# A gated state-space and expert mixer on one core: a new static order, and openings of the inverse that TensorE may run

## The chip, the cores and the metric

The kernel runs on one core of one Trainium2 chip. The metric is device time in microseconds (us) of one execution; lower is better. The core has a matrix engine (TensorE, PE in the profile), a vector engine (VectorE, DVE), an activation engine (ScalarE, ACT), a general engine (GpSimd, POOL), and queues for DMA transfers, of which SyncE's (SP) carries nearly all. Each engine works off its own list of instructions in order and waits on semaphores for what other engines or transfers must deliver first. Operands lie in on-chip memory (SBUF, 128 partitions); matmuls write to PSUM, from which ACT or DVE must take the results away ("evict" them) before the place is used again.

## The reference

For `x = A_u` with 2048 tokens of 512 channels (bf16) the reference mixes two results with a gate per token:

```python
g = sigmoid((x * gate_w).sum(-1))
a = A(x, ...)   # convolution of each channel with a kernel of length 2048, + u * Dskip
b = B(x, ...)   # x, plus an expert's output at the two tokens with the largest score
return g * a + (1 - g) * b
```

In `A` the kernel of channel d is `K[d, l] = Re sum_n C[d,n] * dt[d] * B[d,n] * exp(dt[d] * A[d,n] * l)` with 128 states n; the causal convolution with it is done through FFTs. In `B` a score `x @ w_r` picks two of the 2048 tokens; for these a feed-forward network with 1792 hidden units, `(silu(xs @ w_gate) * (xs @ w_up)) @ w_down`, times the sigmoid of the score, is added to `x`.

## The kernel before

The convolution is done with blocks of 1024 tokens: two blocks of the input, two halves h of the channels (256 each). The stages are:

- `forward(blk)` (L876): transform of a block by matmuls with a table that is loaded from memory, 128 matmuls of 128x512 in 32 operations of four; the results, real and imaginary parts of four frequency tiles, are evicted to `X`.
- `tab1`, `tab2` (L691, L669, L471, L480, L456): for each half, the tables of `exp(dt*A*l)`: an argument by matmul, its fraction, a sine, a magnitude by exponential, and their products. These are DVE and ACT work.
- `kgen(h)` (L905): the kernel in time from these tables, 256 pairs of short matmuls for a half, evicted in pieces by ACT; then three selections (`sel`, L919 to L934) that bring it into the order in which it is transformed.
- `kspec(h)` (L961): the kernel's spectrum, by matmuls with tables `c_ksp` (five of 512 KB for each half), which must land first. In it the block that carries over from the other one is added: for h=0 by TensorE afterwards (L968), for h=1 ahead of the matmuls, either by ScalarE, which writes the scaled copy into PSUM (one ACTIVATE of 128x1024, L949), or by TensorE (two matmuls of 128x512, L968). Which one is a choice per operation.
- `products(h, ...)` (L456): complex products of input and kernel spectra on DVE, with some sums done on TensorE (L1007).
- `inverse(h)`: for each of 16 PSUM groups an opening operation writes `U * (1-g)/g` for two token blocks into PSUM (`sa`, ScalarE, two ACTIVATEs of 128x256, L1036); 16 matmuls (L1053) add the inverse transform of the products; and two evictions (L1061, ACT or DVE) multiply by g and write the output tile.
- `routing()`: transposes of the input (L747), scores (L760), two rounds of argmax with a transpose each for the value and the index (L778, L780), a gather by matmul with one-hot columns (L806), the expert's network with matmuls that have two columns (L824, L837), whose weights share SBUF with other buffers and are loaded late.

The program records 661 operations, an operation being one or several instructions of one engine. Nothing is scheduled at run time: `ORDER` is a string of three base-36 digits for every operation, which gives the order of all of them, and so each engine's list; `SECOND` says for each operation that has two engines as alternatives which one is used; `PLACES` says which PSUM or SBUF place a result takes. The costs beside the operations (`cost=...`) were used when these tables were made, and don't act in the program. A planner's times are therefore not visible in the kernel; its order is. An operation is put on an engine by helpers through which nearly all DVE and ACT work goes: `TT` (L456) two-operand DVE work, `EV` (L475) evictions and copies, `SCL` (L480) scaling, `AC` (L471) an activation function, `CP` (L467) small copies, `DMA` (L483).

Of the kernel before, what the change touches and what calls it, by code (L numbers as in the profile page):

```python
# [356 lines left out]
def small_mats():  # L357
# [14 lines left out]
ORDER = (  # L372
    "00301q00m00x00000200400q00r00s00600701c00500101a01k01b01n01o00h01m00i01l08d01e01d00t04n01v00u00v01y00802001w02108f00w02k08c07602400y00c01f07801u00d009"
    "02e01x02607702502c00z01z02d01002g02l02f02i02702h02j02802a02m00b02b00a07500l01102o02p02901p01s00j02n02q02r02z08e03004o05m01601t03103204p03307903401g04q"
    "03502s03603701707a03802t00g03904b01405l00o00p03n03q01h03b03a07b01203c03d04r07l07n03e03f05s07k01501801303g05n00e00f07m03h03i07c04t03j03k07o04u03r05p05o"
    "03l07p04v03m07q03x04s03y04x04w01901i03v07e07r03w03z05t07d04304107f07g05u04204y04008h07h04405004z05q04907i08g07j0510c10c00c204805w04704607s05200k05307t"
    "05v06004505404c05z05x0610c306705704a07v0c405506300n04d05y0c507u05607w04e03o07z06207x06406r0c906605906s07y0580860ca05b0c604f04i08204h02305a06805c084022"
    "04g04j06t05d05g06901r05e01j06a05h0800c703s08105f06d05i06e06k0c808506l08308906b06f06u05j0cb06v06m08w06n06o0a60cc06w06g0cd06p08b06h05k08y09a08x08706i0bs"
    "09b0880bu08a0a509j09d0bt0bv0ce06509c09e09009h09k08z09f06q06x0bw09g09t09105r09i0bx09209l09m0by09q09p09n09w03t09s02u09r09u0bz06j09v0cf06z09x0a70cg06y03p"
    "03u0ch09o08k07004k04l04m08i0720710ci08j02w0cj0a20ck08l0730cs0a30cm0a009y0a40cl09z0co08r0a109508m0ct08p08n08q0cn02v0cw0a80aa08s0ak0du0930ab0a908t0ac0al"  # L380
    "08o0960cp0ad0am0940ah08u0cq0dv0cr08v0ai0cu0ae0970cy0af0ax0cz0980aj0cv0990d00an0aw0ag0d20d30d50cx0d60d80d90b10dy0d10d40da0db0df0dh0d70dc0de0dd0b20dl0az"
    "02x0di0dx0b30dk0dg0ao0ap0740b40dj0b502y0b70ar0dm0dp0dq0dn0dr0do0b60ds0as06c0b80at0dw0fh0dt0au0av0aq0ff0fi0fr0fj0fk0fg0bd0fs0ba0fm0fn0fl0b90bb0fo0g90be"
    "0b00ga0e10bc0fp0bf0bh0fq0bg0bi0e30ge0gf0bk0ft0gg0gb0gc0e40fu0e80gd0bj0gi0e00bm0fw0ay0bl0g40fv0bn0e20e70gh0dz0ef0ei0ej0eg0e60bo0eq0er0ec0bp0br0eh0e50bq"
    "0e90ek0ep0es0ed0fz0g60ew0ee0ex0g10fx0ev0et0eu0ey0f80ea0gv0fy0hn0f50f60f90fa0f70f20g00ho0hj0gw0gt0ez0hs0hp0g50g20f00g70en0eb0h10h90g80g30f30el0gu0gz0gx"
    "0f10hk0fb0f40gy0h20hc0hl0h00h30h60eo0em0gk0fd0gj0gl0gn0fe0hm0gq0hd0he0hr0hq0ha0h40hx0gm0hb0h50hh0i50gp0i10ht0go0gs0i60gr0i20h70i70hi0hf0h80hg0i30fc0i8"
    "0ib0i40hu0hy0hz0hv0hw0ic0i00ia0i9"
)
# [13 lines left out]
def bass_gated_mix__ssm_conv_s4__moe_arch_mod__prompt_kernel(nc, A_u, A_A_re, A_A_im, A_B_re, A_B_im, A_C_re, A_C_im, A_log_dt, A_Dskip,  # L401
# [24 lines left out]
    with ExitStack() as es:  # L426
# [313 lines left out]
        def routing():  # L740
# [148 lines left out]
        def kgen(h):  # L889
            r = RW[h]  # L890
            for b0, ng in [(8 * i, 8) for i in range(8)]:
# [6 lines left out]
                for g0 in (0, np_):  # L898
                    def mm(hh, b0=b0, gs=range(g0, g0 + np_), pb=pb, np_=np_):
# [246 lines left out]
```

## Time and profile before

| | before |
|---|---|
| median of 3 runs | 151.04 us (150.5 to 151.19) |
| profiled execution | 150.42 us |
| its span, first to last instruction | 148.4 us |
| TensorE busy in the span | 132.8 us, 1723 matmuls |
| VectorE busy | 134.9 us, 199 instructions |
| ScalarE busy | 129.1 us, 210 instructions |
| mean granted TensorE clock | 0.976 of full speed |

The profiled execution is 2.02 us longer than its span, and lies 0.62 us below the median of the three runs. Three engines are busy for between 87% and 91% of the span, so the share of busy time alone doesn't say which of them sets the end; the views below go stage by stage. "Busy" is the union of an engine's instructions. An instruction's mean duration is a little longer than the step from its start to the next one's, since neighbours overlap; the chain of waits gives such steps.

### The profile page before, as it was taken

To read this page: it belongs to the slowest core of one execution; us is meant where nothing else is said; L and a number is where in the kernel's file an instruction comes from. 1 tells how busy PE (TensorE), PEld (TensorE's weight loads), DVE (VectorE), ACT (ScalarE), POOL (GpSimd) and SP (SyncE) were. 2 spreads that over 40 slices of the span, in tenths; PEclk is the share of its full clock that TensorE was granted. 3 is DMA by queue.
4 is the path that set the end of the run, shared out by engine and by line. 5 is a ranking of instruction groups with operands and counts; after the bars stand their busy time and mean duration, and the time that the engine had idled before them with its cause. 6 is when DMAs were issued, how large, how long until landed. Compare 5 with 4: busy or idle time off the path is not lost.

```text
span 148.4 us, 4019 instructions
## 1 busy us (share of the span) xinstructions
PE 132.8 (90%) x1723; PEld 99.8 (67%) x1723; DVE 134.9 (91%) x199; ACT 129.1 (87%) x210; POOL 5.6 (4%) x12
## 2 busy tenths in 40 slices
PE   0289977989999999999969989999999999999980
PEld 0168753766447544997538879968565888888870
DVE  1499999997998999996999999999979999999981
ACT  4689999996699999999998996679899999999540
POOL 8000000000000000000310000010000000000000
PEclk9999999985799999999999999999999999999999
DMA  3899299999700000740080695928800010106216
GB/s 97 265 363 403 94 311 402 406 382 514 324 0 4 0 0 12 246 175 4 0 255 33 181 382 183 383 49 345 325 6 2 4 38 0 35 4 177 84 57 177
DMA packets 13459, 24.93 MB, mean 168 GB/s; under 512 B 1359, under 2 KB 8290, under 8 KB 13282
## 3 DMA queue, kind: packets, MB, share of 16 engines
q1 hardware_dynamic: 12434, 24.03, 45.2%
q10 hardware_dynamic: 976, 0.66, 1.5%
q8 instruction: 13, 0.21, 0.5%
q14 instruction: 4, 0.03, 0.1%
q0 software_dynamic: 32, 0.00, 0.0%
HBM read 22.58 MB, written 4.20 MB: 181 GB/s over the span
## 4 chain that ended last, share of the span: by engine, by line
PE 72%; DMA 17%; DVE 6%; SPq 2%; issue 1%; ACT 0%
PE ps L1053 18%; PE ps L876 16%; PE ps L905 12%; PE ps L961 10%; DMA AR<-in_B_w_up_dram 10%; DMA AR<-c_ksp 5%; PE ps L1007 5%; PE ps L691 3%; DVE AR L456 2%; DMA AR<-in_A_B_im_dram 2%; SPq L483 2%; PE ps L747 2%; PE ps L968 1%; DVE AR L1061 1%; PE ps L760 1%; PE ps L824 1%
## 5 line engine op out<-in xcount | busy, mean ns | idle before, releaser
L456 DVE TENSOR_TENSOR AR<-AR 128x1024 bf16<-128x1024 bf16 (+13 forms) x135 | 118.1, 934 | 5.6 <-DMA AR<-in_A_B_im_dram 2.1
L475 ACT ACTIVATE AR<-ps 128x1024 bf16<-128x1024 f32 (+5 forms) x57 | 46.6, 863 | 5.2 <-PE ps L905 2.3
L876 PE MATMUL ps<-AR 128*128 128x512 bf16 x128 | 31.7, 395 | 0.0
L1053 PE MATMUL ps<-AR 128*128 128x256 bf16 x256 | 29.0, 273 | 0.0
L1053 PEld LDWEIGHTS ps<-AR 128*128 128x128 bf16 x256 | 25.1, 98 | 2.9
L471 ACT ACTIVATE AR<-ps 128x512 bf16<-128x512 f32 (+1 forms) x32 | 24.6, 822 | 2.3 <-PE ps L691 1.4
L876 PEld LDWEIGHTS ps<-AR 128*128 128x128 bf16 x128 | 12.4, 101 | 13.6 <-issue 1.5
L961 PE MATMUL ps<-AR 128*128 128x256 bf16 x160 | 19.3, 273 | 1.8 <-DMA AR<-c_ksp 1.8
L961 PEld LDWEIGHTS ps<-AR 128*128 128x128 bf16 x160 | 15.3, 98 | 5.6 <-DMA AR<-c_ksp 1.6
L905 PEld LDWEIGHTS ps<-AR 128*128 128x128 bf16 x512 | 17.8, 96 | 0.3
L905 PE MATMUL ps<-AR 128*128 128x84 bf16 (+1 forms) x512 | 17.9, 196 | 0.0
L1061 ACT ACTIVATE AR<-ps,AR 128x256 bf16<-128x256 f32 x27 | 11.6, 479 | 3.7 <-PE ps L1053 3.3
L1036 ACT ACTIVATE ps<-AR 128x256 f32<-128x256 bf16 x32 | 14.0, 493 | 0.1
L471 ACT ACTIVATE AR<-AR 128x1024 bf16<-128x1024 int16 (+5 forms) x16 | 12.7, 797 | 0.5 <-DMA AR<-in_A_log_dt_dram 0.3
L691 PE MATMUL ps<-AR 128*128 128x256 bf16 x64 | 10.1, 285 | 0.0
L480 ACT ACTIVATE AR<-ps 128x1024 bf16<-128x1024 f32 x8 | 8.2, 1030 | 0.9 <-PE ps L876 0.8
L591 PE MATMUL ps<-AR 128*128 128x128 bf16 x8 | 2.0, 472 | 7.1 <-DMA AR<-in_A_A_re_dram 4.5
L691 PEld LDWEIGHTS ps<-AR 128*128 128x128 bf16 x64 | 5.7, 99 | 3.2 <-ACT AR L475 0.6
L1007 PE MATMUL ps<-AR 128*128 128x512 bf16 x32 | 7.4, 379 | 0.0
L480 ACT ACTIVATE AR<-AR 128x256 int32<-128x256 f32 (+1 forms) x12 | 6.9, 585 | 0.0
L591 PEld LDWEIGHTS ps<-AR 128*128 128x128 bf16 x8 | 1.1, 170 | 7.6 <-DVE AR L458 4.4
L480 DVE TENSOR_SCALAR AR<-AR 128x256 int32<-128x256 f32 (+1 forms) x18 | 5.7, 327 | 0.4 <-ACT AR L471 0.4
(73 smaller groups left out, 91.3 us busy)
## 6 DMA issues: line engine op xcount, KB each, us to landing
AR<-c_ksp SPq DMA_DIRECT2D x10, 512.0 KB, 4.6
AR<-in_A_u_dram SPq DMA_DIRECT2D x4, 512.0 KB, 6.4
AR<-c_fwd SPq DMA_DIRECT2D x4, 512.0 KB, 11.8
AR<-out_dram SPq DMA_DIRECT2D x4, 512.0 KB, 6.1
AR<-c_inv SPq DMA_DIRECT2D x1, 2048.0 KB, 9.0
AR<-in_B_w_gate_dram SPq DMA_DIRECT2D x1, 1792.0 KB, 10.1
AR<-in_B_w_up_dram SPq DMA_DIRECT2D x1, 1792.0 KB, 14.6
out_dram<-AR SPq DMA_DIRECT2D x14, 128.0 KB, 2.2
```

Source lines behind the costliest of these rows:

```text
L456: return P.op(DVE, lambda h: h.tensor_tensor(out=o, in0=a, in1=b, op=op), rd, wr, cost=tt_cost(o, a, b), **k)
L471: return P.op(ACT, lambda h: h.activation(out=o, in_=a, func=func, scale=scale, bias=bias), rd, wr, cost=0.185 + nel(o) * 0.833e-3 + (0.09 ...
L475: return P.op((ACT, DVE), (lambda h: h.activation(out=o, in_=a, func=ACTF.Copy), lambda h: h.tensor_copy(o, a)), rd, wr, cost=cost or (0.1 ...
L480: return P.op((ACT, DVE), (lambda h: h.activation(out=o, in_=a, func=ACTF.Copy, scale=c), lambda h: h.tensor_scalar(out=o, in0=a, scalar1= ...
L691: last = hh.matmul(pb(0, 128, c * 256, (1, 256)), WP(0, 128, ((2 * h + q) * 4 + c) * 128, (1, 128)), MV(0, 128, a * 512 + f * 256, (1, 256 ...
L876: last = h.matmul(pb(0, 128, part * 512, (1, 512)), F[ft](0, 128, ((par * 4 + st) * 2 + part) * 128, (1, 128)), x, start=(pas + st == 0), ...
L905: last = hh.matmul(pb(0, 128, g // np_ * 512 + g % np_ * W4 + o, (1, n)), TP[h][1 - i // 2](0, 128, (b0 + g) * 128, (1, 128)), r[k](0, 128 ...
L961: last = hh.matmul(pb(0, 128, n * 256, (1, 256)), KP[h][u](0, 128, tau * 128, (1, 128)), KC[h](0, 128, jg * 256, (1, 256)), start=(k == 0 ...
L1007: r = hh.matmul(pb(0, 128, pm * 512, (1, W)), CB(0, 128, 128 * (k if part == 0 else 0), (1, 128)), b(0, 128, ((0, 3), (1, 2))[part][k] * 2 ...
L1036: last = hh.activation(out=pb(0, 128, e * 256, (1, 256)), in_=U(0, 128, tb * D + h * HC, (1, HC)), func=ACTF.Copy, bias=0.0, scale=SG(0, 1 ...
L1053: r = hh.matmul(pb(0, 128, e * 256, (1, 256)), G(0, 128, ((par * 2 + part) * 4 + ft) * 512 + (2 * t2 + e) * 128, (1, 128)), yv(h, blk, par ...
L1061: P.op((ACT, DVE), (lambda hh, o=o, i_=i_, g_=g_: hh.activation(out=o, in_=i_, func=ACTF.Copy, scale=g_), lambda hh, o=o, i_=i_, g_=g_: hh ...
```

## The change

The diff does five things.

1. `ORDER`, `SECOND` and `PLACES` are replaced: every engine gets a new order of its work, some operations with a choice change engines, and some results change places.
2. The planner's costs beside four kinds of operation are other numbers (the transposes of the parameters, 0.66 to 0.25 and 1.7 to 0.55; the short matmuls of `kgen`, 0.0343 to 0.0365 each). They don't act in the program.
3. A buffer `DGX` of 4 KB a partition holds 16 diagonal matrices of 128x128, the identity scaled per token by `(1-g)/g`. One new operation in `late()` writes it: one DVE multiplication (`dgd`) or 16 ACTIVATEs of 128x128 (`dga`).
4. A new small copy in `routing()` puts `(1-g)/g` into bf16 for that.
5. The opening of an inverse group may be done by TensorE (`sp`), with two matmuls that multiply `U` by such a diagonal, as well as by ScalarE (`sa`). Either way the operation now reads `DGX`, so it waits for the new operation of 3.

```diff
-ORDER = ( ... )   # 661 operations
+ORDER = ( ... )   # 663 operations
...
+        DGX = B("dgx", oF + 16 * KB, 4 * KB)
...
-            P.op(PE, pct, [PC, CBI], [bb], cost=0.66)
+            P.op(PE, pct, [PC, CBI], [bb], cost=0.25)
...
-            P.op(PE, wt, [(CM1, p), DG32], [(wp_, p)], cost=1.7)
+            P.op(PE, wt, [(CM1, p), DG32], [(wp_, p)], cost=0.55)
...
+            CP(SGB(0, 128, 64, (1, 16)), SG(0, 128, 96, (1, 16)), [(SG, "x")], [(SGB, "x")])
...
         def late():
+            def dgd(hh):
+                return hh.tensor_tensor(out=DGX(0, 128, 0, (128, 16), (1, 128)), in0=CB(0, 128, 0, (0, 16), (1, 128)), in1=SGB(0, 128, 64, (1, 16), (0, 128)), op=MUL)
+            def dga(hh):
+                r = None
+                for k in range(16):
+                    r = hh.activation(out=DGX(0, 128, k * 128, (1, 128)), in_=CB(0, 128, 0, (1, 128)), func=ACTF.Copy, bias=0.0, scale=SG(0, 128, 96 + k, (1, 1)))
+                return r
+            P.op((DVE, ACT), (dgd, dga), [CBI, (SGB, "x"), (SG, "x")], [DGX], cost=(2.25, 5.2))
...
-                    P.op(PE, mm, kd, [(pb, g0)], cost=np_ * 4 * 0.0343)
+                    P.op(PE, mm, kd, [(pb, g0)], cost=np_ * 4 * 0.0365)
...
-                        P.op(ACT, sa, [(SG, "x")] + [(U, (tb, h)) for tb in tbs(t2, par)], [pb], cost=0.88)
+                        def sp(hh, pb=pb, ts=tbs(t2, par)):
+                            last = None
+                            for e, tb in enumerate(ts):
+                                last = hh.matmul(pb(0, 128, e * 256, (1, 256)), DGX(0, 128, tb * 128, (1, 128)), U(0, 128, tb * D + h * HC, (1, HC)), start=(e == 0), stop=True, ...)
+                            return last
+                        P.op((ACT, PE), (sa, sp), [DGX, (SG, "x")] + [(U, (tb, h)) for tb in tbs(t2, par)], [pb], cost=(0.88, 2 * 0.1095))
```

In the changed kernel lines shift: L691 is L692, L780 is L782, L806 is L808, L824 is L826, L876 is L886, L905 is L915, L919, L931 and L934 are L929, L941 and L944, L961 is L971, L968 is L978, L1036 is L1046, L1061 is L1076. Three places of the order are shown, each before and after.

TensorE from the argmax through the network's first layer, before (L780 transposes of the argmax, L806 the gather, L824 the first layer in two halves, gate then up, each of 56 matmuls; L876 forward transform, L691 arguments, L618 and L631 parameters):

```order
L780 MATMUL ps<-AR 128x128
L876 MATMUL ps<-AR 128x512 x8
L691 MATMUL ps<-AR 128x256 x4
L806 MATMUL ps<-AR 128x2 x64
L876 MATMUL ps<-AR 128x512 x4
L824 MATMUL ps<-AR 128x2 x56
L691 MATMUL ps<-AR 128x256 x4
L824 MATMUL ps<-AR 128x2 x24
L876 MATMUL ps<-AR 128x512 x4
L824 MATMUL ps<-AR 128x2 x32
L691 MATMUL ps<-AR 128x256 x4
L876 MATMUL ps<-AR 128x512 x16
```

The same place now, from the third transpose of the argmax:

```order
L782 MATMUL ps<-AR 128x128
L886 MATMUL ps<-AR 128x512 x12
L619 MATMUL ps<-AR 32x128 x12
L886 MATMUL ps<-AR 128x512 x4
L782 MATMUL ps<-AR 128x128
L886 MATMUL ps<-AR 128x512 x4
L692 MATMUL ps<-AR 128x256 x4
L886 MATMUL ps<-AR 128x512 x4
L808 MATMUL ps<-AR 128x2 x64
L692 MATMUL ps<-AR 128x256 x4
L886 MATMUL ps<-AR 128x512 x4
L826 MATMUL ps<-AR 128x2 x16
```

More groups of the forward transform stand between the transposes, and ahead of the gather and the network; the network's first layer is cut into shorter pieces with forward groups between them.

TensorE where the first half's kernel spectrum begins, before (L931 and L934, L919 and L922 the selections; L961 the spectrum's matmuls, which wait for `c_ksp`):

```order
L876 MATMUL ps<-AR 128x512 x8
L931 MATMUL ps<-AR 32x64 x16
L934 MATMUL ps<-AR 32x64 x8
L919 MATMUL ps<-AR 32x2x64 x32
L922 MATMUL ps<-AR 32x256
L691 MATMUL ps<-AR 128x256 x12
L961 MATMUL ps<-AR 128x256 x32
L691 MATMUL ps<-AR 128x256 x4
L961 MATMUL ps<-AR 128x256 x36
L968 MATMUL ps<-AR 128x512 x2
```

and now:

```order
L941 MATMUL ps<-AR 32x64 x16
L944 MATMUL ps<-AR 32x64 x8
L929 MATMUL ps<-AR 32x2x64 x16
L932 MATMUL ps<-AR 32x256
L692 MATMUL ps<-AR 128x256 x16
L971 MATMUL ps<-AR 128x256 x32
L692 MATMUL ps<-AR 128x256 x8
L971 MATMUL ps<-AR 128x256 x32
```

Four matmuls more of the arguments stand before the first wait for `c_ksp`, four more before the second, and behind the 64 spectrum matmuls come 16 short matmuls of the second half's `kgen` (L915), ahead of the four that read the last table.

ScalarE from the second half's selections to the first openings, before (L475 evictions, 128x672 those of `kgen`, L949 the carries, L1036 the openings):

```order
L475 ACTIVATE AR<-ps 128x672 x8
L475 ACTIVATE AR<-ps 128x512 x2
L475 ACTIVATE AR<-ps 128x256
L475 ACTIVATE AR<-ps 128x1024 x3
L949 ACTIVATE ps<-AR 128x1024
L475 ACTIVATE AR<-ps 128x1024 x2
L949 ACTIVATE ps<-AR 128x1024
L475 ACTIVATE AR<-ps 128x1024 x2
L1036 ACTIVATE ps<-AR 128x256 x2
```

and now:

```order
L475 ACTIVATE AR<-ps 128x672 x5
L475 ACTIVATE AR<-ps 128x1024
L475 ACTIVATE AR<-ps 128x512 x2
L862 ACTIVATE AR<-AR 128x128 x16
L475 ACTIVATE AR<-ps 128x1024 x5
L1046 ACTIVATE ps<-AR 128x256 x2
L475 ACTIVATE AR<-ps 128x1024 x2
L1046 ACTIVATE ps<-AR 128x256 x2
L475 ACTIVATE AR<-ps 128x1024
L959 ACTIVATE ps<-AR 128x1024
```

The new operation (L862) stands between the eviction of the selections and the evictions of the second half's spectrum. In the whole order all 16 openings (32 ACTIVATEs) are on ScalarE, and no matmul reads `DGX`; two of the four carries are on TensorE.

More of the change, by code (lines that the diff above doesn't have):

```diff
@@ L377 @@
[L377 to L384, printed above, removed]
@@ new lines @@
+    "03303401r00k00b04r06801f03500l02t06703604s01h03701j07b03803904y03a02u03o05t03c03b02w07c05u03r03d07g04w03e07d03f06905v06a03g01q07f05x03h04x07e08d07h03i"
+    "04t05w01701807i06b05y04d03j03k07j06c04z05m03l07o03m05103n05n03x07l07k07n07m03y05203z05000e03w08i05305z06107p04000o04403p07q05402v06005o05502x043042056"
+    "01907r08f05805q0bu0bw0bx06207s00p04a04503s04905704804704b0bv03t05p04602305a06307u0by04e0590bz07t05b0c006z03u05r06406503q07004f04c07w04i04h07v04g05c0cc"
+    "04j04k0ca05d07x06s0cb05f06t07y07105e0c105g0c906u05j06l08008705h07z06m03v0820830cd06n07208105i0ce08506w06v06x08607307408408g06o05k06p09b08a09e05l09c08b"
@@ new lines @@
+    "0cf0c409f06q09i0cg09h08c06f0c309d02209k09g09j0c208j08l09l08k08m08806e0c509m0c608909q09n09o09p0a909t0a80c709u08h08n06g06r09r08o09w05s0a708p09x06h09v09s"
+    "09y0c804l06y0ch0ci02y0ck0cj04m06i06j0a10a30a40dw09z0a50960a008q0a208r0cl08s0cm0cn08t0co09408u0a60cw08v0cq0950cx0ad0970ae0an0ao08w0cr0980cp0cs08x08z0aa"
+    "0ab0900ct04n0ay09908y0cu0ac0cv0al0d109a0am0af0ag0d20as0at0910d50ah0920cy0d40930ai0d00cz0aj0au0ak0d80d70d90d30db0da06k0dk0dd0de0dc0dj0az0dg0dh02z0d60dy"
+    "0dn0df0b40dl0di0dz0dm0do0ap0aq0dp0e00b30dr0ar0dq0aw0750dt0b50du0dx0b60b70ds0dv0b90b80av0ft0fj0fh0ax0fk0ba0bc0fi0fu0fl0fm0fo0660fp0bf0fn0fq0b006d0bb0bd"
@@ new lines @@
+    "0e30be0bg0bh0b20fr0gb0gg0gd0e20b10gc0bj0fs0gh0fy0bi0e40gi0ge0gf0bk0e90eh0fz0e10g10bl0ei0bm0e50e70eb0et0hm0e80ej0ec0ev0gk0ee0ef0bn0hs0g00bo0e60ea0ek0g3"
+    "0ew0f00fv0bp0gj0fw0br0bq0ed0eg0er0g20en0bs0es0eu0ez0fx0bt0el0ex0g60g40gv0gx0g80ep0ey0f40f10em0gw0fa0gy0f50f70f20fb0f80f90fc0fd0g70g50h10eo0h30fg0h20g9"
+    "0ga0h80hb0hp0hq0f30gz0hn0ho0h00hc0hd0hl0h50h60h90eq0h40ht0hr0gl0hh0ff0hu0he0h70hf0hg0hk0f60fe0ha0hj0gm0gn0hi0gp0gr0go0i30gs0hv0hz0gq0i70gu0i80i90ia0gt"
+    "0i40i50id0i00i60i10i20ie0hw0hx0ib0hy0ic"
@@ L394 @@
+    "000000000000000000000000000000000000000000000000100000000000000000000000000000000000000000000000000000000000000100100000000000000000000000000000000000"
+    "000000000000000000000000000000000000000000000110010001000000000"
 )
 PLACES = (
-    "01423133616317223004222300044046004104604640220001010461601600022426024665444046640000062000001002460240676276454015064006020202260217635402"
+    "01063504132271425444111000060166160100462222460101000461201640640460640606722660022000040000001004026462001647654706266220222002042025363140"
@@ L1037, in sa @@
                             return last
-                        P.op(ACT, sa, [(SG, "x")] + [(U, (tb, h)) for tb in tbs(t2, par)], [pb], cost=0.88)
+                        def sp(hh, pb=pb, ts=tbs(t2, par)):
+                            last = None
+                            for e, tb in enumerate(ts):
+                                last = hh.matmul(pb(0, 128, e * 256, (1, 256)), DGX(0, 128, tb * 128, (1, 128)), U(0, 128, tb * D + h * HC, (1, HC)), start=(e == 0), stop=True, skip_group_check=(e > 0))
+                            return last
+                        P.op((ACT, PE), (sa, sp), [DGX, (SG, "x")] + [(U, (tb, h)) for tb in tbs(t2, par)], [pb], cost=(0.88, 2 * 0.1095))
                         for e, tb in enumerate(tbs(t2, par)):
```

16 lines of the change are left out of this document (5 added, 11 removed).

## The prediction

> **What bounds the kernel now.** I read the page's summary first, then busy time by stage, then the chain of waits and the idle times on PE and DVE.
>
> ```profile
> span 148.4 us, 4019 instructions
> PE 132.8 (90%) x1723; PEld 99.8 (67%) x1723; DVE 134.9 (91%) x199; ACT 129.1 (87%) x210; POOL 5.6 (4%) x12
> PE 72%; DMA 17%; DVE 6%; SPq 2%; issue 1%; ACT 0%
> ```
>
> PE and DVE are busy about equally, and the chain that ended last runs mostly over PE. That would call PE the bound. The stages show a second one (the columns are stretch and length, then busy time and instructions of PE, PEld, DVE, ACT and POOL, then the granted clock and DMA):
>
> ```profile
> core 0: us, PE busy (x) PEld busy (x) DVE busy (x) ACT busy (x) POOL busy (x), PEclk, DMA share, GB/s
> 6.04:32.00 25.96, 21.92 (x356) 16.40 (x357) 25.56 (x63) 25.12 (x45) 0.00 (x0) 1.00 0.90 335
> 32.00:36.00 4.00, 3.54 (x58) 2.01 (x57) 3.52 (x5) 3.82 (x6) 0.00 (x0) 0.50 1.24 465
> 36.00:40.00 4.00, 4.00 (x25) 1.94 (x23) 3.69 (x5) 2.13 (x3) 0.00 (x0) 0.65 1.00 423
> 40.00:72.00 32.00, 32.00 (x432) 21.35 (x431) 30.14 (x46) 31.14 (x46) 0.00 (x0) 1.00 0.16 53
> 72.00:100.00 28.00, 26.19 (x489) 21.51 (x487) 27.94 (x38) 23.86 (x33) 2.13 (x2) 1.00 0.56 193
> 100.00:142.39 42.39, 42.39 (x358) 34.66 (x357) 41.13 (x41) 38.66 (x73) 0.00 (x0) 1.00 0.26 92
> ```
>
> From 6.04 us on, DVE's idle time in these rows is 0.40 + 0.48 + 0.31 + 1.86 + 0.06 + 1.26 = 4.37 us in 136.35. The larger pieces by name, with the first and the last long stretch:
>
> ```profile
> 6.04 2.56 DVE L456 TENSOR_TENSOR AR<-AR 128x1024 f32<-128x1024 bf16 x3 [2.10 <-DMA AR<-in_A_B_im_dram]
> 36.31 2.36 DVE L456 TENSOR_TENSOR AR<-AR 128x2048 bf16<-128x2048 bf16 x2 [0.79 <-PE ps L824]
> 46.35 0.43 DVE L480 TENSOR_SCALAR AR<-AR 128x1024 bf16<-128x1024 bf16 x1 [0.39 <-ACT AR L471]
> 67.90 4.10 DVE L456 TENSOR_TENSOR AR<-AR 128x2048 bf16<-128x2048 bf16 x4 [1.47 <-ACT AR L471]
> 108.74 2.29 DVE L456 TENSOR_TENSOR AR<-AR 128x4096 bf16<-128x4096 bf16 x1 [0.63 <-ACT AR L475]
> 111.36 31.03 DVE L456 TENSOR_TENSOR AR<-AR 128x1024 bf16<-128x1024 bf16 x34 [0.33 <-ACT AR L475]
> ```
>
> DVE's last product ends at 111.36 + 31.03 = 142.39, and the last matmuls, evictions and stores take the remaining 6.0 us of the span. Any gain on PE alone would end in waits for products. So the time is DVE's: 6.04, its work, its waits, and the tail of 6.0.
>
> PE has more to give back. Its waits, and then the rows with half the clock beside the same work at full clock:
>
> ```profile
> 20.53 0.33 PE L780 MATMUL ps<-AR 128*128 128x128 f32 x1 [0.72 <-DVE AR L778]
> 23.35 0.33 PE L780 MATMUL ps<-AR 128*128 128x128 f32 x1 [0.82 <-ACT AR L778]
> 32.91 0.80 PE L824 MATMUL ps<-AR 128*128 128x2 bf16 x24 [0.46 <-DMA AR<-in_B_w_up_dram]
> 77.75 3.67 PE L961 MATMUL ps<-AR 128*128 128x256 bf16 x32 [1.30 <-DMA AR<-c_ksp]
> 85.83 0.60 PE L961 MATMUL ps<-AR 128*128 128x256 bf16 x4 [0.49 <-DMA AR<-c_ksp]
> ```
>
> ```profile
> 33.72 1.73 PE ps L876 x4
> 36.28 0.88 PE ps L691 x4
> 37.15 4.35 PE ps L876 x16
> 56.32 3.45 PE ps L876 x16
> 59.77 0.44 PE ps L691 x4
> 86.43 0.43 PE ps L968 x2
> ```
>
> At the full clock four forward matmuls take 3.45 / 4 = 0.86 us and four argument matmuls 0.44. The half clock cost 0.87 + 0.44 + 0.90 = 2.2 us, between 32 and 39 us, the stretch with the two-column matmuls of the network and the wait for its weights. A rule of the Trainium skill bears on this ("TensorE: Matmul & The Clock Gate", "What's actually happening"): the clock is halved after a window of about 3.4 us that was idle, and the windows run freely, so that their phase shifts from run to run. The trace agrees with half clock, not with an idle window: PE's longest pause there is 0.46 us, so a low share of real streaming seems to be enough.
>
> **The change, part by part.** Durations of what moves (busy, mean ns of one):
>
> ```profile
> L475 DVE COPY AR<-ps 128x1024 bf16<-128x1024 bf16 x6 | 3.8, 688 | 0.0
> L480 DVE TENSOR_SCALAR AR<-AR 128x256 int32<-128x256 f32 x13 | 3.6, 289 | 0.0
> L480 DVE TENSOR_SCALAR AR<-AR 128x1024 bf16<-128x1024 bf16 x5 | 2.1, 425 | 0.4 <-ACT AR L471 0.4
> L458 DVE TENSOR_TENSOR AR<-AR 128x512 f32<-128x512 f32 x2 | 1.3, 686 | 0.0
> L669 DVE TENSOR_SCALAR AR<-AR 128x1024 int32<-128x1024 int32 x2 | 1.4, 690 | 0.2 <-ACT AR L471 0.2
> L467 DVE CAST AR<-AR 128x16 bf16<-128x16 f32 x1 | 0.2, 167 | 0.0
> L778 ACT ACTIVATE AR<-AR 128x128 f32<-128x128 f32 x1 | 0.4, 393 | 0.0
> L949 ACT ACTIVATE ps<-AR 128x1024 f32<-128x1024 bf16 x4 | 4.5, 1133 | 0.0
> L1036 ACT ACTIVATE ps<-AR 128x256 f32<-128x256 bf16 x32 | 14.0, 493 | 0.1
> ```
>
> *Openings.* The new order leaves all sixteen on ScalarE: 0 us, on either engine. What is left of that part is the operation that writes the diagonals, now ahead of the openings.
>
> *Diagonals.* 16 ACTIVATEs of 128x128. The only row of that size is 393 ns, 6.3 us for 16. Neighbours overlap: the openings' 14.0 us for 32 make 0.44 each where one lasts 0.493, so I take 0.393 less 0.055, 0.34 each, 5.4 us; bounds 4.5 (if the overlap is as large as on DVE, 0.1) and 6.3. They stand where ScalarE would have taken up the second half's spectrum. PE has, behind the selections, matmuls for its free PSUM places: three groups of 16 L961 matmuls (16 x 0.11 = 1.75 each, from four in 0.44) and one of eight, 6.1 us. ScalarE needs 0.6 + 5.4 for an eviction and the diagonals and some 1.0 for the first spectrum eviction: 7.0. PE waits 0.9 us there, up to 1.8 with 6.3. PE comes to that place early, so DVE sees little of it.
>
> *Carries.* Two leave ScalarE (2 x 1.13 = 2.3 us) and become four matmuls of 0.215 on PE, 0.86 us.
>
> *DVE's added work*, from start to start, so some 0.09 under the means: the cast of the parameters (512, f32) 0.60, one more transposed-input eviction (1024) 0.60, a shift of 128x768 instead of ScalarE's (three quarters of 0.69) 0.50, an eviction of 128x256 0.33 (between 0.29 and 0.42), the scaling of the fourth argmax transpose 0.20, five small casts and scalings some 0.10 each, 0.49. Taken off: three scalings of 128x256 at 0.22 and one of 128x1024 at 0.34. Sum 2.72 - 1.00 = +1.7, with rounding on both sides +1.8. A cast of 512 more, 0.34, lies in the wait for B_im ahead of 6.04; if that cover is gone it costs 0.34. One output eviction goes back to ScalarE behind the last product. So without any change of waits: +1.8 us at the end.
>
> *DVE's waits.* The 0.79 at 36.31 is the wait for the network's first layer, itself late by PE's 0.46 and by the half clock (0.83 us for four matmul pieces ahead of it). The order now does the gather later, with forward groups ahead and between, and the weights land while PE has other work. A wait of about 0.5 stays, for DVE's cast of the hidden values behind 64 two-column matmuls. The 1.47 at 67.90 is for ScalarE's sine behind `kgen`'s evictions; it becomes about 0.7, as these are reached earlier by what PE saves. The others (0.40 + 0.39 + 0.96 and small ones) shrink to some 0.6, as ScalarE loses 2.3 us of carries and 2.5 us of moved work. That is 1.8 us of 4.37; 2.55 goes. Bounds: none left (4.37 goes), or all stay.
>
> *PE's waits.* The transposes' 0.72 and 0.82 lie behind forward groups now, 1.5 us; the 0.46 for the weights too; of the 1.30, 0.44 is covered by four argument matmuls; the 0.49 by sixteen short `kgen` matmuls. With the half clock gone, PE gains 2.2 + 1.5 + 0.46 + 0.44 + 0.49 - 0.86 = 4.2 us, more than DVE can follow. What is late next is DVE: PE will wait in the products and the inverse for what it saved.
>
> *Sum.* +1.8 of work, -2.55 of waits: -0.75 on DVE's last product; the tail the same. Profile 150.42 - 0.75 = 149.67. It lies 0.62 under the median of the runs, so 150.3 us for the median.
>
> **The rivals.**
>
> *The half clock comes back* (B). For it: two-column matmuls now stand among forward groups, but the gather and the second layer are still 64 and 56 in a row. Against: the piece of 56 and 24 is cut up. Price: 2.2 us on PE, of which DVE sees about the wait for the network again (0.79 - 0.5) and half the 0.7 saved on the sine, and the spectrum later by some 1: DVE +1.2. Then 151.5. The clock row decides, and where in PE's run it falls.
>
> *The diagonals weigh on ScalarE* (C). At 6.3 us, and if PE has not got ahead, 1.8 us of PE's wait comes through to the products, about +1.5 against the forecast: 151.8.
>
> *DVE is the bound and its waits stay* (D). Then the added 1.8 us are paid: 150.42 + 1.8 + 0.62 = 152.8, slower than before. It is one mechanism: each wait that I let shrink is for ScalarE's or PE's result, and DVE's own order, which is fuller early, may just meet them at another place. It decides where more than 2.55 of the 4.37 us stay. For it: DVE's waits were for ACT twice in the largest rows, and ScalarE gets 5.4 us more.
>
> *All of DVE's waits go* (E). 1.8 - 4.37 = -2.6: 148.5. For it: PE gains 4.2 in my count, and early. Against: a sine and its consumer are ordered on different engines.
>
> *That the change doesn't do what it says* is so for the openings, as the order shows; it has no time of its own beside C.
>
> **How the numbers follow.** Chances: forecast 0.40 (between 149.6 and 151.0), B 0.20, C 0.10, D 0.15, E 0.15. About 0.5% (0.75 us) is what a measurement of this kernel can tell from no change: 151.04 - 0.75 = 150.29, so the forecast lies at the edge, half of it faster. Faster: half of 0.40, most of E, and a little of the others where PE's gain is larger than I let it be: 0.45. Same (150.29 to 151.8): the other half, most of B, half of C: 0.33. Slower: D, the rest of C and of B: 0.22. The range runs from 148.4 (E) to 152.5, just under D; the forecast's own is 149.6 to 151.0.
>
> **What would show each step.** The granted clock at 1.0 throughout after 12 us, or a stretch of 0.5 (B). DVE idle after its first long stretch near 1.8 us, against 2.55 or more (D). The L862 row near 5.4 us, against 6.3 (C), with a wait of PE for ScalarE's eviction of about 0.9 behind it. PE's L782 rows without waits. DVE busy near 136.5 us (134.9 + 1.8 + 0.34 - 0.48 for the output eviction of 0.48 that leaves it). The prediction is wrong if DVE stands in longer waits than 1.8 us in the products while PE runs, for then PE is the bound after all, or if the last product ends before 140.

## The result, and the profile after

The changed kernel takes 148.97 us (median of 4 runs, 148.83 to 149.28) where the kernel before takes 150.77 (4 runs, 150.2 to 151.19): a ratio of 0.9886 with a 95% interval of 0.9845 to 0.9927. That is 1.8 us less; the forecast was 150.3 against a median of 151.04, 0.75 us less. The two profiled executions differ by 1.14 us (149.28 against 150.42). Here and below a ratio is taken over the quicker executions of each kernel, so it can lie off the ratio of the medians. Four lines of the changed kernel's page:

```profile
span 147.2 us, 4041 instructions
PE 132.7 (90%) x1727; PEld 100.8 (68%) x1727; DVE 135.9 (92%) x205; ACT 129.8 (88%) x219; POOL 6.1 (4%) x12
PEclk9999999999999999999999999999999999999999
PE 44%; ACT 23%; DVE 23%; DMA 4%; SPq 2%; issue 2%
```

The stretch of half clock is gone, and the chain that ended last is now shared by three engines. The same stages as before (columns as in the prediction; the last product ends at 141.17 here):

```profile
6.04:32.00 25.96, 23.63 (x260) 16.77 (x260) 24.71 (x65) 23.82 (x41) 0.00 (x0) 1.00 0.90 333
32.00:36.00 4.00, 4.00 (x93) 3.11 (x92) 4.00 (x10) 3.92 (x6) 0.00 (x0) 1.00 1.03 420
36.00:40.00 4.00, 4.00 (x107) 3.28 (x105) 3.98 (x6) 3.97 (x10) 0.00 (x0) 1.00 1.21 462
40.00:72.00 32.00, 31.90 (x479) 21.20 (x478) 31.78 (x49) 31.84 (x46) 2.06 (x1) 1.00 0.25 79
72.00:100.00 28.00, 26.09 (x443) 21.91 (x442) 27.88 (x34) 25.77 (x42) 0.52 (x1) 1.00 0.56 195
100.00:141.00 41.00, 41.00 (x341) 32.88 (x339) 40.76 (x41) 36.95 (x75) 0.00 (x0) 1.00 0.19 66
```

DVE's idle time in them is 1.25 + 0 + 0.02 + 0.22 + 0.12 + 0.24 = 1.85 us, where it was 4.37. Its longer waits, and then TensorE's:

```profile
16.24 1.29 DVE L475 COPY AR<-ps 128x1024 bf16<-128x1024 bf16 x2 [0.88 <-PE ps L748]
22.90 0.69 DVE L670 TENSOR_SCALAR AR<-AR 128x1024 int32<-128x1024 int32 x1 [0.24 <-ACT AR L471]
44.49 0.29 DVE L480 TENSOR_SCALAR AR<-AR 128x256 int32<-128x256 f32 x1 [0.19 <-ACT AR L471]
```

```profile
9.93 3.60 PE L748 MATMUL ps<-AR 128*128 128x128 bf16 x32 [2.02 <-DMA AR<-in_A_u_dram]
17.59 0.55 PE L761 MATMUL ps<-AR 128*128 128x2 bf16 x16 [0.16 <-DVE AR L475]
89.13 4.55 PE L915 MATMUL ps<-AR 128*128 128x84 bf16 x128 [0.34 <-DVE AR L456]
96.64 1.92 PE L971 MATMUL ps<-AR 128*128 128x256 bf16 x16 [0.82 <-ACT AR L475]
98.95 3.67 PE L971 MATMUL ps<-AR 128*128 128x256 bf16 x32 [0.40 <-DVE AR L456]
```

The waits of the argmax, of the weights and of `c_ksp` are gone from TensorE's list, or under 0.2 us. New ones stand at the start, where the first transposes take 3.60 / 32 = 0.112 us each, and between 89 and 99 us. From 98.95 us on TensorE waits for nothing, as before it did from 85.83 on.

A ledger of TensorE from the two traces, in us, to its last matmul (144.14 before, 142.93 after):

| | before | after | gain |
|---|---|---|---|
| idle before 10 us (inputs) | 7.14 | 7.93 | -0.8 |
| the 64 input transposes | 4.21 | 5.51 | -1.3 |
| half clock, 32 to 39 us | 2.2 | 0 | +2.2 |
| waits at the argmax, the weights, `c_ksp` and two small ones | 4.09 | 0.16 | +3.9 |
| waits for DVE and ACT, 72 to 99 us | 0 | 1.70 | -1.7 |
| the two carries | 0 | 0.86 | -0.9 |

The lines sum to +1.4; the ends differ by 1.21, the rest is in small pieces. Some 6 us were won in the middle, and nearly 5 given back: at the start, for the carries, and to two engines that are as full.

The two lines of the start can't be put down to the order. They differ from one execution to the next, in both kernels. The scores that follow the last input transposes begin at 16.49 us here, but at 15.70 in a second trace of the changed kernel (e0 below, no edit, 148.53 us); in the kernel before they begin at 15.27, but at 16.83 in a trace with an edit that acts only much later (e8). The rows of e0 and of e8:

```profile
15.70 0.94 PE L761 MATMUL ps<-AR 128*128 128x2 bf16 x32
```

```profile
16.83 1.74 PE L760 MATMUL ps<-AR 128*128 128x2 bf16 x64
```

In e0 VectorE's wait of 0.88 us is 0.23, and TensorE's last wait ends at 98.17 us instead of 98.95. So the execution profiled above was 0.75 us longer than e0's by its start alone:

```profile
15.45 1.29 DVE L475 COPY AR<-ps 128x1024 bf16<-128x1024 bf16 x2 [0.23 <-PE ps L748]
```

```profile
98.17 3.67 PE L971 MATMUL ps<-AR 128*128 128x256 bf16 x32 [0.40 <-DVE AR L456]
```

ScalarE has 23% of the chain in the first trace, all of it between 20 and 67 us, and 10% in e0's. No run took work off it there, so whether it limits that stretch is open.

### The profile page after: what moved, and what is told of

It reads as the page before. It is cut to its first block, busy times and chain, and to the rows that moved or that the text cites. A ratio compares the mean times of both kernels' runs of the same rounds, so it can differ in the third digit from the quotient of the medians.

```text
span 147.2 us, 4041 instructions
## 1 busy us (share of the span) xinstructions
PE 132.7 (90%) x1727; PEld 100.8 (68%) x1727; DVE 135.9 (92%) x205; ACT 129.8 (88%) x219; POOL 6.1 (4%) x12
## 4 chain that ended last, share of the span: by engine, by line
PE 44%; ACT 23%; DVE 23%; DMA 4%; SPq 2%; issue 2%
DVE AR L456 20%; PE ps L1068 18%; ACT AR L471 11%; ACT AR L480 6%; PE ps L886 5%; PE ps L971 5%; PE ps L1017 5%; ACT AR L475 4%; DMA AR<-in_A_u_dram 4%; PE ps L748 4%; SPq L483 2%; ACT AR L670 2%; PE ps L692 2%; DVE AR L1076 1%; DVE AR L475 1%
## 5 line engine op out<-in xcount | busy, mean ns | idle before, releaser
L456 DVE TENSOR_TENSOR AR<-AR 128x1024 bf16<-128x1024 bf16 (+10 forms) x135 | 117.4, 931 | 0.3
L475 ACT ACTIVATE AR<-ps 128x1024 bf16<-128x1024 f32 (+5 forms) x55 | 45.6, 881 | 4.1 <-PE ps L915 1.4
L886 PE MATMUL ps<-AR 128*128 128x512 bf16 x128 | 30.8, 379 | 0.1
L1068 PE MATMUL ps<-AR 128*128 128x256 bf16 x256 | 28.9, 273 | 0.0
L1068 PEld LDWEIGHTS ps<-AR 128*128 128x128 bf16 x256 | 25.0, 98 | 3.2
L971 PE MATMUL ps<-AR 128*128 128x256 bf16 x160 | 19.6, 273 | 1.3 <-ACT AR L475 0.8
L915 PEld LDWEIGHTS ps<-AR 128*128 128x128 bf16 x512 | 18.6, 97 | 2.4 <-issue 0.4
L886 PEld LDWEIGHTS ps<-AR 128*128 128x128 bf16 x128 | 11.8, 98 | 11.7 <-ACT AR L480 0.8
L915 PE MATMUL ps<-AR 128*128 128x84 bf16 (+1 forms) x512 | 19.2, 196 | 0.4 <-DVE AR L456 0.3
L971 PEld LDWEIGHTS ps<-AR 128*128 128x128 bf16 x160 | 15.0, 98 | 4.5 <-ACT AR L475 1.2
L1076 ACT ACTIVATE AR<-ps,AR 128x256 bf16<-128x256 f32 x28 | 12.1, 467 | 3.5 <-PE ps L1068 3.3
L1046 ACT ACTIVATE ps<-AR 128x256 f32<-128x256 bf16 x32 | 13.6, 473 | 0.1
L692 PE MATMUL ps<-AR 128*128 128x256 bf16 x64 | 9.1, 273 | 0.1
L480 ACT ACTIVATE AR<-AR 128x256 int32<-128x256 f32 (+1 forms) x16 | 9.1, 592 | 0.0
L748 PE MATMUL ps<-AR 128*128 128x128 bf16 x64 | 5.9, 273 | 2.0 <-DMA AR<-in_A_u_dram 2.0
L1017 PE MATMUL ps<-AR 128*128 128x512 bf16 x32 | 7.6, 380 | 0.0
L692 PEld LDWEIGHTS ps<-AR 128*128 128x128 bf16 x64 | 5.7, 97 | 2.8 <-ACT AR L475 0.6
L592 PE MATMUL ps<-AR 128*128 128x128 bf16 x8 | 1.9, 489 | 5.9 <-DVE AR L458 5.9
L748 PEld LDWEIGHTS ps<-AR 128*128 128x128 bf16 x64 | 5.4, 128 | 2.2 <-DMA AR<-in_A_u_dram 2.1
```

The costliest lines, as they stand in the source:

```text
L456: return P.op(DVE, lambda h: h.tensor_tensor(out=o, in0=a, in1=b, op=op), rd, wr, cost=tt_cost(o, a, b), **k)
L475: return P.op((ACT, DVE), (lambda h: h.activation(out=o, in_=a, func=ACTF.Copy), lambda h: h.tensor_copy(o, a)), rd, wr, cost=cost or (0.1 ...
L480: return P.op((ACT, DVE), (lambda h: h.activation(out=o, in_=a, func=ACTF.Copy, scale=c), lambda h: h.tensor_scalar(out=o, in0=a, scalar1= ...
L692: last = hh.matmul(pb(0, 128, c * 256, (1, 256)), WP(0, 128, ((2 * h + q) * 4 + c) * 128, (1, 128)), MV(0, 128, a * 512 + f * 256, (1, 256 ...
L748: last = h.transpose(bb(0, 128, db * 256 + t_ * 128, (1, 128)), U(0, 128, (2 * q + t_) * D + db * 128, (1, 128)), IDN(0, (1, 128)))
L886: last = h.matmul(pb(0, 128, part * 512, (1, 512)), F[ft](0, 128, ((par * 4 + st) * 2 + part) * 128, (1, 128)), x, start=(pas + st == 0), ...
```

## The experiments

Each run was measured beside the kernel before. Runs e0 to e3 are one series, e4 to e7 another on the same chip, e8 to e11 a third on another chip. Within a series the medians can be set side by side, across series only roughly. The medians of the kernel before are 151.39, 151.43 and 151.34 us in the three.

**The changed kernel again (e0).** No edit.

> The changed kernel again, as the base of the runs beside it. By its first comparison 0.9886 of the kernel before, 148.97 us. Both theories say the same here: about 149.0 us, the profile without a stretch of half clock.

149.11 us (12 runs, 148.53 to 149.71) against 151.39, ratio 0.9945 (0.9905 to 0.9985). The kernel before was run 29 times in this series, and one thing stood out: its time goes with the mean granted clock of the execution. Over the three series, 51 executions of it:

| mean clock of the execution | executions | median us | range |
|---|---|---|---|
| 0.996 and 0.998 | 2 | 148.29 | 148.16, 148.42 |
| 0.98 to 0.99 | 23 | 150.71 | 149.63 to 152.24 |
| 0.97 to 0.98 | 26 | 151.93 | 150.21 to 153.86 |
| changed kernel, 0.997 to 1.000 | 16 | 149.1 | 148.53 to 149.71 |

In the two executions where the half clock stays away, the kernel before is not slower than the changed one. Both are in this series, which brings the ratio nearer to 1 than the medians are (0.985). There is no trace of the two.

**One diagonal (e1).** 15 of the 16 ACTIVATEs of L862 are left out; nothing reads them.

```diff
-                for k in range(16):
+                for k in range(1):
```

> The changed kernel with one of the sixteen diagonals written, so 15 ACTIVATEs of 128x128 less on ScalarE (4.8 us of L862 become 0.3); nothing reads the others. Theory DVE (VectorE's work and waits set the end, the diagonals are hidden): 149.0, between 148.7 and 149.2. Rival ACT (the diagonals delay the spectrum's evictions and so the products): 147.5 to 148.2. The trace of the changed kernel shows a wait of PE ahead of the spectrum (0.82 us) for an eviction that ends before the diagonals begin, which speaks for the first.

149.31 us (148.6 to 149.97) against 149.11, no gain: ratio 0.9972 (0.992 to 1.0023). The diagonals cost what this row of the changed kernel's groups shows, on ScalarE alone:

```profile
L862 ACT ACTIVATE AR<-AR 128x128 bf16<-128x128 bf16 x16 | 4.8, 399 | 0.0
```

In e1's trace TensorE waits the same 0.82 us ahead of the spectrum, so that wait isn't theirs; it is for the eviction of the selections ahead of them. Rival C falls: the diagonals take 4.8 us, not 6.3, and their price doesn't show.

**More of VectorE's work, first try (e2 on the changed kernel, e4 on the kernel before).** One multiplication of 128x2048 more ahead of the first product, into a free place.

```diff
+                more = (h, blk, qds[0]) == (0, 1, 0)
...
+                        hh.tensor_tensor(out=UO(0, 128, 0, (1024, 2), (1, 2 * W)), in0=X(0, 128, xo(blk, 0, 0), (2048, 2), (1, 2 * W)), in1=KK[h](0, 128, q0, (2048, 2), (1, 2 * W)), op=MUL)
```

> The changed kernel with one more DVE multiplication of 128x2048 (about 1.2 us from such rows) ahead of the first product of the first half, near 91 us, written to a place that nobody reads. Theory DVE: VectorE has no wait behind this place, so the whole of it comes through: +1.1 to +1.2, 150.2. Theory PE (TensorE sets the end from the second half's spectrum on): only what exceeds its reserve; PE waits for VectorE there already (0.40 us at 98.95), so it comes through too, +1.0 to +1.2. Neither: 0.

> The kernel before with one more DVE multiplication of 128x2048 (about 1.2 us) ahead of the first product, near 90 us, written to a place that nobody reads. Theory DVE (as the prediction put it, VectorE's work and waits set the end before as well): +1.1 to +1.2, 152.0. Theory PE (in the kernel before TensorE runs without a wait from 85.83 us on and sets the end; VectorE still waits 0.63 and 0.33 us at 108.74 and 111.36): what exceeds these 0.96 us, 0 to +0.4, 151.0 to 151.2.

160.92 us (160.15 to 161.98) and 160.09 (158.51 to 161.16), ratios 1.0758 (1.0654 to 1.0861) and 1.0559 (1.0503 to 1.0616). These are badly made: the place was not yet free. The rows of e2 and of e4:

```profile
100.78 1.23 DVE L1009 TENSOR_TENSOR AR<-AR 128x2048 bf16<-128x2048 bf16 x1 [9.47 <-ACT AR L862]
```

```profile
98.26 1.23 DVE L999 TENSOR_TENSOR AR<-AR 128x2048 bf16<-128x2048 bf16 x1 [7.51 <-PE ps L961]
```

VectorE waited for the diagonals that are written there, or for the last reader of a table, and all behind it with it. They say only that a stall of 8.7 to 10.7 us on VectorE comes through, in both kernels, and nothing of a small one. The test was made again (e8, e9).

**More of TensorE's work late (e3).** Four matmul pairs of the sums at L1017 are done twice.

```diff
-                                for k in range(2):
+                                for kk, k in enumerate((0, 0, 1) if i == 0 else (0, 1)):
...
-... start=(i + k == 0), stop=(i + k == 2))
+... start=(i + k == 0), stop=(i + k == 2 or (i, kk) == (0, 0)))
```

> The changed kernel with the first matmul pair of four sums on TensorE done twice (L1017, eight matmuls of 128x512 more at 0.215 us, 1.7 us between 102 and 113 us; the result is the same). Theory DVE: PE saved more than DVE could follow, so it has room: 0 to +0.4, 149.0 to 149.4. Theory PE: it runs without any wait from 98.95 us to its end, so all of it comes through: +1.5 to +1.7, 150.6.

150.83 us (150.16 to 151.11) against 149.11: +1.72 for 1.72 us of work; ratio 1.0094 (1.0039 to 1.0149). VectorE now waits where it didn't:

```profile
114.90 27.25 DVE L456 TENSOR_TENSOR AR<-AR 128x4096 bf16<-128x4096 bf16 x31 [1.03 <-PE ps L1017]
```

The traces, free of what the start does, agree: from the end of its last wait to its last matmul TensorE takes 45.64 us here (98.81 to 144.45) and 43.98 in the changed kernel (98.95 to 142.93; in e0 and e1 43.98 as well), +1.66. TensorE has no room behind 99 us in the changed kernel. That it had saved more than VectorE can follow was wrong there.

**The kernel before at full clock (e5).** One forward group and one argument group are done twice, so that more real streaming, that is matmuls with many columns, lies among the two-column matmuls.

```diff
-                        for st in range(4):
+                        for st in (list(range(4)) * (2 if (blk, ft, pas, part) == (0, 1, 0, 1) else 1)):
...
-                            for c in range(4):
+                            for c in (list(range(4)) * (2 if (h, q, a, f) == (0, 0, 1, 0) else 1)):
```

> The kernel before with more real streaming between 28.6 and 32 us: one forward group at 29.4 us and one argument group at 31.7 us are done twice (0.86 + 0.44 = 1.3 us more of TensorE's work, the result is the same). If too little streaming halves the clock, the stretch at 32 to 39 us goes back to full clock. Theory DVE: PE gains 2.2 - 1.3 + 0.46 (the wait for the weights is filled) = 1.4 us, VectorE follows by what its waits at 36.31 and 67.90 shrink: -0.3 to -0.8. Theory PE: -1.0 to -1.4. If the clock isn't governed by streaming: half clock stays, +0.8 or more.

With 1.3 us more of work the kernel is faster: 150.34 us (148.54 to 151.7) against 151.43, ratio 0.99 (0.9843 to 0.9958). Its windows and its chain of waits:

```profile
32.00:36.00 4.00, 4.00 (x96) 3.39 (x94) 3.65 (x6) 4.00 (x7) 0.00 (x0) 1.00 1.33 496
36.00:40.00 4.00, 4.00 (x23) 1.97 (x22) 4.00 (x5) 3.39 (x6) 0.00 (x0) 1.00 0.94 396
```

```profile
34.06 0.88 PE ps L876 x4
36.19 3.45 PE ps L876 x16
```

The same groups that took 1.73 and 4.35 us take 0.88 and 3.45. All six executions have a mean clock of 0.994 or more, where the eleven of before beside them have 0.977 to 0.985. The edit also removes the wait of 0.46 us for the weights, a rival for the cause; but in the trace of before the granted clock is 1.00 up to 32.00 us and 0.53 and 0.50 in the two quarters of a microsecond behind it, while the wait lasts from 32.46 to 32.91, and TensorE shows no pause between 23.4 and 32.46. So the half clock came ahead of that wait, and too little streaming among the short matmuls is the cause that is left. How little is enough, and which of the two repeated groups mattered, was not separated. Four of the six took 150.3 to 151.7 us in spite of the clock; there is no trace of these, and what they lost is open.

**Openings on TensorE (e6).** The eight openings of the second half use what the change makes possible.

`SECOND` goes from 0 to 1 for the operations 607, 608, 609, 611, 633, 634, 635 and 637.

> The changed kernel with the second half's eight openings on TensorE, as the change allows: 16 matmuls of 128x256 (1.75 us) for 16 ACTIVATEs of 128x256 (about 7 us). Theory DVE: ScalarE isn't needed there and PE has room: 0 to +0.3. Theory PE: +1.4 to +1.8, or more where an opening waits on TensorE's list for a place in PSUM that isn't evicted yet.

151.79 us (150.8 to 153.31), ratio to the kernel before 1.002 (0.9968 to 1.0072), where the changed kernel's were 0.9886 and 0.9945: the gain is gone. It was not run in one series with the changed kernel, so the size by the medians, +2.7 us, is rough. In the traces TensorE takes 46.05 us from its last wait to its last matmul (99.36 to 145.41) instead of 43.98, +2.07 for 1.75 us of matmuls; the sign agrees with e3.

**Carries back on ScalarE (e7).**

`SECOND` goes from 1 to 0 for the operations 561 and 564.

> The changed kernel with the two carries back on ScalarE: four matmuls of 128x512 less (0.86 us), two ACTIVATEs of 128x1024 more (2.3 us), in the stretch behind the diagonals. Theory DVE: 0, or up to +1 if ScalarE's lateness reaches the products. Theory PE: -0.8 if ScalarE can take them, else the delay of ScalarE shows as waits of PE at L971: up to +1.5.

152.75 us (152.41 to 154.13), ratio 1.011 (1.0063 to 1.0156), more than either theory gave. TensorE waits for the carries, which ScalarE reaches only behind the diagonals and three evictions, and at 106.4 us, around the second of these waits, the clock falls to half:

```profile
105.52 0.61 PE L971 MATMUL ps<-AR 128*128 128x256 bf16 x4 [2.02 <-ACT ps L959]
106.56 1.03 PE L971 MATMUL ps<-AR 128*128 128x256 bf16 x4 [0.42 <-ACT ps L959]
```

```profile
104.00:108.00 4.00, 2.05 (x10) 1.19 (x11) 4.00 (x2) 3.82 (x5) 0.00 (x0) 0.80 0.09 34
108.00:112.00 4.00, 4.00 (x20) 1.94 (x18) 2.44 (x2) 2.91 (x5) 0.00 (x0) 0.78 0.00 0
```

A clock of 0.80 and 0.78 over 8 us is 1.7 us of full clock. So it seems that the diagonals are hidden only because the first two carries left ScalarE; the carries on ScalarE without the diagonals were not run.

**A small piece of VectorE's work (e8 on the kernel before, e9 on the changed one with one diagonal).** The same multiplication, one product later, where the place is free (the lines show the difference from e2 and e4).

```diff
-                more = (h, blk, qds[0]) == (0, 1, 0)
+                more = (h, blk, qds[0]) == (0, 1, 1)
```

> The kernel before with one more DVE multiplication of 128x2048 (1.23 us) ahead of the second pair's first product, at 100.9 us, where it waits for nothing. Theory DVE (VectorE's work and waits set the end, as the prediction put it): +1.1 to +1.2. Theory PE (TensorE, which runs without a wait from 85.83 us on, sets the end, and VectorE has its later waits of 0.63 and 0.33 us to spare): 0 to +0.4. Theory both (the two are tied: the sums on TensorE wait for the products, and the last matmuls for the last product): +1.1 to +1.2 with a new wait of PE at its sums or at the end.

> The changed kernel with one diagonal instead of sixteen and the same additional DVE multiplication (1.23 us) at the same product, at 100.2 us. Against the run with one diagonal alone (149.3 us): theory DVE and theory both +1.1 to +1.2, 150.5; theory PE (TensorE sets the end alone from 98.95 us on): 0 to +0.3, 149.4.

The kernel before shows no cost: 151.11 us (148.72 to 152.91) against 151.34, ratio 0.9904 (0.9823 to 0.9985). The spread is wide, 4.2 us over six executions, and the interval rests on two of them, so the times alone don't exclude +1.2. The traces decide it. From the end of its last wait to its last matmul TensorE takes 58.32 us here and 58.31 in the kernel before, where that wait ends at 85.83:

```profile
86.49 0.60 PE L961 MATMUL ps<-AR 128*128 128x256 bf16 x4 [0.66 <-DMA AR<-c_ksp]
139.41 5.40 PE L1060 MATMUL ps<-AR 128*128 128x256 bf16 x48
```

```profile
138.74 5.40 PE L1053 MATMUL ps<-AR 128*128 128x256 bf16 x48
```

So nothing of the 1.23 us reaches TensorE. VectorE has no wait between 68 and 144 us, so the 0.63 and 0.33 us of before took most of the work up:

```profile
68.40 4.10 DVE L456 TENSOR_TENSOR AR<-AR 128x2048 bf16<-128x2048 bf16 x4 [1.43 <-ACT AR L471]
144.05 1.79 DVE L1068 TENSOR_SCALAR AR<-ps,AR 128x256 bf16<-128x256 f32 x4 [0.47 <-ACT AR L1068]
```

The changed kernel takes 150.30 us (149.94 to 150.8), against 149.31 with one diagonal in another series: +1.0 for 1.23, ratio 0.9948 (0.9908 to 0.9988). TensorE has a new wait at its sums:

```profile
103.64 1.04 PE L1024 MATMUL ps<-AR 128*128 128x512 bf16 x4 [1.19 <-DVE AR L456]
```

From the end of its wait at 98.78 us to its last matmul at 143.97 TensorE takes 45.19 us here and 43.98 in the changed kernel, +1.2 (the last groups here and there):

```profile
135.07 8.90 PE L1075 MATMUL ps<-AR 128*128 128x256 bf16 x80
```

```profile
134.03 8.90 PE L1068 MATMUL ps<-AR 128*128 128x256 bf16 x80
```

So before, TensorE set the end from 85.83 us on and VectorE had some 1 us to spare; after, they are tied.

**An early start (e10), and with less of VectorE's work (e11).** 14 transposes of the identity fill TensorE's wait for the first tile. e11 also has one diagonal, and the eviction of the last selection on ScalarE.

```diff
+                for _ in range(14):
+                    h.transpose(w8(0, 128, 128, (1, 128)), IDN(0, (1, 128)), IDN(0, (1, 128)))
```

In e11 also `range(16)` becomes `range(1)` as in e1, and `SECOND` of the operation 498 goes from 1 to 0.

> The changed kernel with 14 transposes of the identity ahead of the small transpose at 7.7 us, where TensorE else waits 2.0 us for the first input tile; their result is not used. The transposes that follow take 0.112 us each until 13.5 us and 0.062 after. Theory start: TensorE is throttled at first and wakes after some 3.4 us of work, so the transposes run at 0.062 from about 10 us, VectorE's wait of 0.88 us at 16.24 shrinks to 0 to 0.2, and the whole schedule behind it comes earlier: -0.4 to -0.9, 148.3 to 148.6. Rival transfers: the tiles arrive no faster than the transposes take them, 0.

> The same early work, one diagonal instead of sixteen, and the eviction of the second half's last selection (128x256, 0.43 us on VectorE at 96.82) on ScalarE, which has room where the diagonals were. Theory both: VectorE loses 0.35 us where it has no wait, and the wait of TensorE for VectorE at 98.95 (0.40 us) goes with it: -0.35 beside the early gain, 147.9 to 148.3. Theory PE alone: -0.4 more from the wait of TensorE. Theory without a gain at the start: 148.7.

e10 is inconclusive: 150.23 us (148.55 to 151.98), ratio 0.9887 (0.9826 to 0.9947). The profiled execution, one of the long ones, shows what was meant, transposes at 1.75 / 24 = 0.073 us and no wait of VectorE at 16 us, but also a pause of TensorE that no other trace here has, with no releaser to be seen, and half clock behind it (0.64 in 44 to 48 us; two of the six executions have a mean clock of 0.983 and 0.986):

```profile
10.50 1.75 PE L748 MATMUL ps<-AR 128*128 128x128 bf16 x24 [0.31 <-DVE AR L467]
42.57 0.28 PE L692 MATMUL ps<-AR 128*128 128x256 bf16 x1 [2.14 <-issue]
```

e11 takes 148.30 us (148.15 to 149.57) against 151.34: ratio 0.9826 (0.9782 to 0.987), the fastest version here, some 0.8 us under the changed kernel by their medians in different series. VectorE's 0.88 us and TensorE's 0.40 are gone from its trace; TensorE's 0.82 is 1.10. Which of its three edits carries the gain was not separated. Beside e0's trace (148.53 us), where the transposes end as early without any edit (15.70 against 15.67 us), e11's profiled execution (148.16) is 0.4 us shorter, about what was expected of VectorE's part.

## Why the prediction was right or wrong

- **"The time is DVE's" is the step that failed, for the kernel before.** VectorE's waits were read as costs, but VectorE had room: 1.23 us more on it moved TensorE's last matmul by 0.01 us, counted from TensorE's last wait (58.32 against 58.31, e8). The time was TensorE's, which ran without a wait from 85.83 us to its last matmul; what mattered was how early it got there. The full page had said so with its chain, 72% on TensorE and 17% on transfers, most of which waited for TensorE.
- **For the changed kernel** the claim is half right: VectorE is at its limit (e9, +1.0 for 1.23), but TensorE is too (e3, +1.72 for 1.72). That TensorE gains 4.2 us, more than VectorE can follow, held for the last forward group, which ends at 69.65 us instead of 73.73; from there on it waits for VectorE and ScalarE, 1.70 us in all. The 2.1 us lost at the start (a later first tile and slow first transposes) were not in the sum; they vary from one execution to the next (e0 has the scores 0.8 us earlier).
- **The half clock: cause right, price perhaps too small.** It was priced at 2.2 us on TensorE, of which 1.2 at the end if it came back (rival B). In the kernel before the step between the two large groups of executions is 1.2 us; against the two at full clock it is 150.71 - 148.29 = 2.4 us for a mean clock of 0.98 to 0.99 and 3.6 for 0.97 to 0.98, of which the start may have a part. It did not come back in 16 executions of the changed kernel, but with transposes put ahead (e10) two of six have a mean clock of 0.983 and 0.986 again. By the two executions at full clock the half clock would be the whole of the gain (148.29 against 149.1); four of e5 at full clock, with 1.3 us of repeated work, took 150.3 to 151.7 us and don't bear that out. How much of the gain is the order's own is open.
- **VectorE's added work**, +1.8 us: measured from 6.04 us on, it is 133.28 - 131.98 = 1.30. The cast of the parameters was priced by a two-operand row (0.69); it took 0.43:

```profile
L475 DVE CAST AR<-AR 128x512 bf16<-128x512 f32 x1 | 0.4, 428 | 0.0
```

- **VectorE's waits**, 1.8 us left: 1.85 are left, but at other places, so the match is luck. 0.88 is for the input transposes, a wait that was not foreseen and that is 0.23 in e0's trace; those forecast behind the network and the sine are nearly gone.
- **The diagonals**, 5.4 us with bounds of 4.5 and 6.3: 4.8, and no cost at the end (e1). TensorE's wait of 0.9 us there came out at 0.82, but for another reason, the eviction ahead of them. That they seem to need the carries on TensorE (e7) was missed.
- **The openings**: nothing was moved, as the order showed, and moving eight of them costs time (e6).
- **The sum**, -0.75 us, against -1.14 between the profiles and -1.8 between the medians. Its sign was right, and the time lies inside the range of 148.4 to 152.5, but under the forecast's own 149.6 to 151.0. In VectorE's own sum the waits shrank by 2.52 us (2.55 forecast) and the work rose by 1.30 (1.8), so its last product ends at 141.17 instead of 142.39, 1.22 us earlier. The sum came near because the end of VectorE's last product lies at the same distance ahead of TensorE's last matmul in both kernels (1.75 and 1.76 us), not because VectorE set it: the half clock was counted as VectorE's waits, and TensorE's start and its waits at 72 to 99 us were left out. Rival D fell (VectorE's waits did not stay). Rival E's time (148.5) is nearer to the median than the forecast, but not its reason, since 1.85 us of VectorE's waits are left.

## What to carry to other kernels

Before an engine without idle time is called the bound, follow a wait of its partner to what comes last: an engine that is 91% busy may be keeping step with another. A small piece of extra work on each engine in turn (1 to 2 us, result unchanged) tells which one sets the end, if the place that it writes is truly free. Counting in the traces from one engine's last wait to its last instruction shows differences of 0.1 us where the times of the runs spread over several. And look at the granted clock of each execution before comparing orders of work: here a short stretch of two-column matmuls cost TensorE 2.2 us.

## What was not expected of the hardware

- **More work made the kernel faster.** 1.3 us of repeated matmuls among two-column ones took the half clock away (e5), with windows of 0.50 and 0.65 back at 1.00. TensorE never paused there for more than 0.46 us, and that pause came behind the fall of the clock, so "busy" on the page is not what the clock follows. The Trainium skill, "TensorE: Matmul & The Clock Gate", section "What's actually happening", names an idle window of about 3.4 us as the cause; here a stretch mostly of two-column matmuls was enough, and in e7 two pauses of 2.02 and 0.42 us.
- **The first transposes are slow though the clock row says 1.00.** 0.112 us each up to 13.5 us, 0.062 later; with matmuls ahead of them 24 take 1.75 us. The trace's clock record begins only at 14.31 us, with the full clock, so the 1.00 ahead of it is no measurement; in e0 it begins at 12.83. The same section's some 3.4 us of work until the full clock is near these rows: the first transposes begin 4.4 us ahead of it here and 4.1 in e0. A mean clock under 1 need not be a loss either: the record of e0 (0.998) ends with half clock from 145.95 us on, behind its last matmul at 142.15.
- **Times of one kernel lie in steps**: the mean clock of the kernel before takes values near 0.977, 0.984 and, twice in 51, 0.997, with medians 1.2 and 2.4 us apart. The trace at 0.976 has 6.83 us of half clock in one piece (32.01 to 38.84), e8's at 0.985 has 3.41 (35.37 to 38.78), so the step is one such piece more or less. What decides between them from one execution to the next, no run here shows.
